# A gated delta rule kernel with a softplus feed-forward: contiguous inverses, queries in longer runs, raw keys and separate key products in chunks 2 and 3, unread products, another order of work

## The chip, the cores and the metric

The kernel runs on one core of a Trainium2 chip. The metric is the device time of one execution in microseconds (us). The core has five engines that run their own instruction streams and wait for each other by semaphores: TensorE (PE in the profile; PEld is its weight load), VectorE (DVE), ScalarE (ACT), GpSimd (POOL) and SyncE (SP), which issues transfers only.

## The reference

Four batches, eight heads (32 streams), 768 steps, head dimension 48. Each stream keeps a 48 x 48 state. Its output is the x of a feed-forward layer with 384 inputs and 2048 hidden units over 3072 tokens.

```python
def _attn_ref(q, k, v, beta, g):
    B, H, S, D = q.shape                      # 4, 8, 768, 48
    k_n = k / (np.linalg.norm(k, axis=-1, keepdims=True) + 1e-06)
    state = np.zeros((B, H, D, D))
    for t in range(S):
        readout = np.einsum('bhd,bhde->bhe', q[:, :, t], state)
        y[:, :, t] = g[:, :, t] * readout
        v_old = np.einsum('bhde,bhd->bhe', state, k_n[:, :, t])
        state = state + beta[:, :, t, None, None] * np.einsum('bhd,bhe->bhde', k_n[:, :, t], v[:, :, t] - v_old)

def _moe_ref(x, w_in, w_out):                 # x: 3072 x 384, w_in: 384 x 2048
    h = x @ w_in
    return (np.maximum(h, 0) + np.log1p(np.exp(-np.abs(h)))) @ w_out
```

## The kernel before, in words

The 768 steps are cut into 12 chunks of 64. Inside a chunk the recurrence becomes matrix products and the inverse of a triangular matrix of 64 x 64 per stream; from chunk to chunk only the state goes on. Chunks are handled in pairs (`GROUPS`): 0 and 1, 2 and 3, up to 10 and 11.

**Loads.** `load` fetches k, q, v and g of a chunk in two transfers each (`k1.0` is chunk 1, batches 0 and 1; `k1.1` is batches 2 and 3), 192 KB each. A partition is a time step, so DRAM is read in runs of 48 floats, 192 bytes. All go through SP's queue, but for `k0.1` and `k1.1`, which ACT issues. The feed-forward weights come through POOL's queue (`wload`, `w0.*` and `w1.*`).

**Front.** Keys and queries become half precision (`cast`). From the second pair on, `unit` (L284) multiplies each key by its inverse norm instead, and so waits for `norms`: ACT squares (`ksq`), DVE sums (`red`), a root follows (ACT for pairs 0 and 2, POOL's power for the others, L481), and DVE takes the reciprocal (`rnorm`). TensorE transposes (`trs`, L312) and ACT or DVE bring the result into `kqt` (`kev`). `gram` (L419, L420) forms key-key and key-query products of one batch half together; ACT or DVE takes the key part out (`kkc`), DVE masks the query part (`mask`). In chunks 0 and 1, whose keys stay raw, two items do it: `gramk` (L349, L350) and, when q is there, `gramq` (L382). There `lbeta` folds the norms into beta, and `vs` (L704) scales the values in the chain.

**Inverse.** For a pair, `ln` (L521) transposes on DVE, `prep` (L536) scales, and fifteen `step`s of two instructions each (L544, L551) solve 16 x 16 blocks: on DVE for pair 0, on POOL for all others. `c16` casts the result, `tn` (L564) and two `t32` (L574) transpose it on DVE, and TensorE builds the 32 x 32 blocks from it (`xmm` L598, `xs`, `tmm` L619 and L625, `td2`). The inverse lies in `td` as 32 rows of 32 heads, [P, i, u]: the elements of one head are 32 elements apart. `zmm` (L651, L658) makes the 64-row part `z` of it, with `td` as the moving operand.

**Chain.** Per chunk and half m of the heads: `ks` and `qs` (products with the state, L696), `w` (values minus that, DVE), `umm` (L737, L741; the stationary operand of L741 is one head of `td`), `u1`, `zu` (L762), `u2`, `smm` (L782) into the next state (`s`, DVE), `ymm` (L812), `y` (times g, DVE), `ytr` (L844) and `xt`, which lays the result out as x.

**Dense.** For each job (chunks 0, 1, then pairs 2-3 to 8-9, then 10, 11), `g1` (L872) makes 128 hidden units by 256 or 512 tokens, `soft` (L884, ACT) applies the softplus into a `ga` buffer, `g2` (L899) accumulates 128 tokens by 384 outputs over 16 blocks, `o` copies them out of the one buffer `p_o`, and `store` sends them off.

**Order.** Nothing is scheduled at run time. Every piece is an item with a number, its engines and what it depends on; the table `_ORDER` is a list of words like `D131` (item 131 on DVE). Each engine does its items in the order of the table, and waits in it block what follows on the same engine. Buffers come from rings of fixed size (`r_k` 4, `r_ga` 17, `p_d` 5 banks of PSUM, and others), and the table's order decides who gets which.

Read out by names, the table before begins on three engines like this:

```
SP:   k1.0 k0.0 q1.1 k2.0 q0.0 q1.0 k2.1 q0.1 k3.0 g1.1 v0.0 v0.1 q2.1 q2.0 k3.1 q3.1 q3.0 v1.0 q5.0 g0.1 g0.0 g1.0 v1.1 ...
ACT:  ... xs:0 w0:0.0 kev:q2.1 td2:0 ksq:3 z:0 u1:0.0 sqrt:2 u2:0.1 cast:qn3.0 ...
POOL: kn0.1 kn0.0 qn1.1 qn1.0 vs:0 w0:0.1 w0.0 clear:4 w0.2 vs:1 unit:kn2 clear:2 diag:2 w0.1 w0.3 unit:kn3 w1.0 diag:4 w1.1 w1.2 w1.3 qn4 prep:2 step:2 x15 unit:kn5 unit:kn4 sqrt:6 ...
```

Of the kernel before, what the change touches and what calls it, by code (L numbers as in the profile page):

```python
# [10 lines left out]
F32 = mybir.dt.float32  # L11
# [5 lines left out]
GROUPS = [[c, c + 1] for c in range(0, 12, 2)]  # L17

# [59 lines left out]
def kernel(  # L78
# [11 lines left out]
    nc = tc.nc  # L90
# [37 lines left out]
    r_q = ring("qf", 2, [P, 2, H, D], F32)  # L128
# [3 lines left out]
    r_qn = ring("qn", 2, [P, 2, H, 64], F16)  # L132
    r_ksq = ring("ksq", 1, [P, 2, H, D], F32)
    r_nv = ring("nv", 3, [P, 32], F32)
    r_nl = ring("nl", 2, [P, 32], F32)
    r_bl = ring("bl", 3, [P, 32], F32)
    r_kk = ring("kk", 3, [P, 2, U, HC], F16)
    r_kqt = ring("kqt", 10, [P, 2 * NP * 2 * C + HC], F16)
# [8 lines left out]
    r_td = ring("td", 4, [P, HC, U], F16)  # L147
# [6 lines left out]
    r_ga = ring("ga", 17, [P, 512], F16)  # L154
# [9 lines left out]
    for t in r_kn.tiles + r_qn.tiles:  # L164
        nc.vector.memset(t[:, :, :, D:], 0.0)
    for r in range(2):
# [27 lines left out]
    for t in r_kqt.tiles:  # L194
        nc.vector.memset(t[:, 4 * NP * C :], 0.0)
# [27 lines left out]
    def load(name, x, r, c, b2):  # L223
# [4 lines left out]

        def fn(en):
# [8 lines left out]
            add("load", f"{name}{c}.{b2}", "A" if name == "k" and c < 2 and b2 else "S", fn,  # L238
                bufs=[b])
# [26 lines left out]
    def kq_of(c, p):  # L266
        return kqt[c, p].ap[:, : 4 * NP * C].rearrange("p (n t) -> p n t", n=2 * NP)

    def front(c, kk, nv, nv_it):
        cl = c % 2  # L270
        parts = 2 if c < 2 else 1
        for p in range(2):
            kqt[c, p] = Buf(r_kqt)
        its, x_of = {}, {}
        for name, ring_ in (("k", r_kn), ("q", r_qn)):
# [3 lines left out]
            for h in range(parts):  # L279
                sl = slice(h, h + 1) if parts == 2 else slice(0, 2)  # L280
                if name == "k" and nv is not None:

                    def unit(en, f=f, x=x):
# [15 lines left out]
                        lambda en, f=f, x=x, sl=sl: copy(en, x.ap[:, sl, :, :D], f.ap[:, sl]),  # L299
                        deps=fl, bufs=[f, x], size=768 // parts)  # L300
# [3 lines left out]
            for h in range(parts):  # L304
# [3 lines left out]
                def trs(en, x=x, tp=tp, ps=ps):  # L308
                    o = f16ps(tp.ap).rearrange("p (a n t) -> p a n t", a=2, n=NP)
                    for p in ps:  # L310
                        for i in range(NP):
                            nc.tensor.transpose(  # L312
                                o[:, p, i],
                                x.ap[:, p, 2 * i : 2 * i + 2].rearrange("p h d -> p (h d)"),
                                ident,
                            )
# [4 lines left out]
                for p in ps:  # L321

                    def kev(en, p=p, tp=tp, name=name):
                        s = f16ps(tp.ap).rearrange("p (a n t) -> p a n t", a=2, t=C)[:, p]
                        kq = kq_of(c, p)
                        copy(en, kq[:, :, :C] if name == "k" else kq[:, :, C:], s)

                    its[name].append(
                        add("kev", f"{name}{c}.{p}", "AD", kev, deps=[t1], bufs=[tp, kqt[c, p]])
# [9 lines left out]
        if c < 2:  # L339
# [697 lines left out]
```

## Time and profile before

| | |
|---|---|
| three runs | 281.72, 284.75, 284.81 us; median 284.75 |
| the profiled execution | 282.21 us |
| its span, first to last instruction | 280.3 us |
| granted TensorE clock | 0.994 |
| busy: PE, PEld, DVE, ACT, POOL | 238.7, 165.1, 153.7, 130.2, 114.1 us |
| transfers | 107705 packets, 27.71 MB, 99 GB/s on average |
| SP's queue | 101600 packets, 23.21 MB, 51.1% of the time of 16 DMA engines |

The span is what the trace covers; 1.9 us of the execution lie around it. The busy time of PE counts overlapping products once. The chain of waits names what ended last before each instruction; an idle engine matters only where it stands in that chain or where PE, the busiest engine, waits for it.

### The profile page before, as it was taken

The numbers are of one execution on the slowest core, as the hardware profiler recorded it, in microseconds if no ns is written. First come the engines' busy times: TensorE is split into PE (matmuls) and PEld (weight loads), VectorE is DVE, ScalarE is ACT, GpSimd is POOL, SyncE is SP. The second block draws the span as 40 slices with busy tenths as digits, with TensorE's granted clock in tenths as the row PEclk, the third lists the DMA queues.
The fourth block names the chain that finished last, engine by engine and source line by source line (L and its number), as shares of the span: only waits on it lengthen the run. The fifth ranks groups of instructions, "written<-read, shape, count | busy, mean of one in ns | idle before, by whom it ended". The sixth has DMA issues, their size and how long they took to land.

```text
span 280.3 us, 13451 instructions
## 1 busy us (share of the span) xinstructions
PE 238.7 (85%) x6112; PEld 165.1 (59%) x6112; DVE 153.7 (55%) x333; ACT 130.2 (46%) x248; POOL 114.1 (41%) x217
## 2 busy tenths in 40 slices
PE   0540579979978998899998999999999999999993
PEld 0420467857647673467765657756566566677761
DVE  7899645482266787856684585561764242413000
ACT  3551265364374677563414755126652355214630
POOL 8115019308805888988605527820038600000000
PEclk9999999999979999999999999999999999999999
DMA  8999968999972399921885980510233410110123
GB/s 120 157 149 148 196 100 133 190 185 177 164 121 39 59 166 151 175 51 35 142 143 90 147 165 21 131 33 5 60 59 68 102 33 5 30 30 4 28 56 87
DMA packets 107705, 27.71 MB, mean 99 GB/s; under 512 B 100864, under 2 KB 107648, under 8 KB 107648
## 3 DMA queue, kind: packets, MB, share of 16 engines
q1 hardware_dynamic: 101600, 23.21, 51.1%
q0 software_dynamic: 3968, 3.25, 7.7%
q8 instruction: 48, 0.79, 1.3%
q10 hardware_dynamic: 2080, 0.39, 1.0%
q14 instruction: 9, 0.07, 0.1%
HBM read 25.26 MB, written 4.72 MB: 107 GB/s over the span
## 4 chain that ended last, share of the span: by engine, by line
PE 50%; POOL 21%; DVE 13%; issue 13%; ACT 2%; POOLq 0%; DVEq 0%
PE h L872 15%; PE o L899 13%; POOL tt L551 8%; POOL tmp L544 8%; PE d L696 3%; DVE ln L521 3%; PE d L658 2%; POOL kn L284 2%; PE d L312 2%; PE d L741 2%; PE d L625 2%; PE d L812 2%; PE d L762 2%; DVE tmp L544 2%; POOL nn L536 2%
## 5 line engine op out<-in xcount | busy, mean ns | idle before, releaser
L884 ACT ACTIVATE ga<-h 128x512 f16<-128x512 f32 x96 | 55.7, 598 | 46.3 <-PE h L872 44.5
L872 PE MATMUL h<-xt,w_in 128*128 128x512 f16 (+1 forms) x384 | 75.3, 331 | 1.9 <-ACT ga L884 1.9
L899 PE MATMUL o<-w_out,ga 128*128 128x384 f16 x384 | 73.3, 332 | 0.6 <-ACT osb L205 0.6
L899 PEld LDWEIGHTS <-ga 128*128 128x128 f16 x384 | 35.6, 99 | 24.0 <-issue 2.4
L872 PEld LDWEIGHTS <-w_in 128*128 128x128 f16 x384 | 35.0, 99 | 21.7 <-issue 2.7
L551 POOL TENSOR_TENSOR tt<-tt,tmp 128x30 f32<-128x30 f32 (+7 forms) x75 | 27.6, 368 | 5.9
L544 POOL TENSOR_TENSOR tmp<-nn,tt 128x30 f32<-128x30 f32 (+7 forms) x75 | 26.9, 359 | 5.8
L207 DVE CAST u<-d 128x384 f16<-128x384 f32 x21 | 11.5, 555 | 22.7 <-PE d L741 9.0
L536 POOL TENSOR_TENSOR nn<-ln,beta_l 128x256 f32<-128x256 f16 x10 | 6.3, 650 | 40.4 <-DVE ln L521 40.2
L481 POOL TENSOR_TENSOR nv<-nv,half_c 128x32 f32<-128x32 f32 x3 | 16.5, 5504 | 12.8 <-DVE nv L468 12.8
L207 DVE COPY osb<-o 128x384 f32<-128x384 f32 x12 | 6.6, 548 | 27.4 <-PE o L899 27.4
L205 ACT ACTIVATE kqt<-d 128x512 f16<-128x512 f16 x26 | 15.2, 595 | 13.8 <-DVE kqt L207 10.4
L205 ACT ACTIVATE u<-d 128x384 f16<-128x384 f32 x27 | 12.9, 489 | 17.6 <-PE d L741 10.2
L284 POOL TENSOR_TENSOR kn<-kf,nv 128x768 f16<-128x768 f32 x10 | 14.7, 1475 | 14.3 <-DVE nv L491 10.6
L437 DVE TENSOR_TENSOR mt<-d,mask 128x256 f16<-128x256 f32 x40 | 15.8, 417 | 7.2 <-PE d L420 3.7
L827 DVE TENSOR_TENSOR yg<-d,gf 128x384 f16<-128x384 f32 x24 | 12.9, 553 | 8.5 <-PE d L812 7.5
L312 PE MATMUL d<-ident,kn 128*128 128x128 f16 x96 | 9.1, 250 | 8.7 <-DVE kn L207 7.6
L598 PE MATMUL d<-tn,kk 16*32 16x16 f16 x768 | 7.3, 184 | 10.6 <-DVE tn L564 10.4
L696 PEld LDWEIGHTS <-kqt 48*64 48x64 f16 x704 | 12.7, 112 | 5.8 <-issue 4.6
L696 PE MATMUL d<-s,kqt 48*64 48x48 f16 x704 | 15.4, 192 | 0.5 <-issue 0.5
L205 ACT ACTIVATE kk<-d 128x256 f16<-128x256 f32 x33 | 11.3, 384 | 8.3 <-DVE mt L437 4.1
L564 DVE STREAM_TRANSPOSE tn<-tw 128x512 f16<-128x512 f16 x6 | 8.7, 1454 | 11.3 <-POOL tw L207 9.1
(106 smaller groups left out, 399.1 us busy)
## 6 DMA issues: line engine op xcount, KB each, us to landing
qf<-in_q_dram SPq DMA_DIRECT2D x24, 192.0 KB, 5.5
gf<-in_g_dram SPq DMA_DIRECT2D x24, 192.0 KB, 4.5
vf<-in_v_dram SPq DMA_DIRECT2D x24, 192.0 KB, 5.4
out_dram<-osb SPq DMA_DIRECT2D x48, 96.0 KB, 2.2
kf<-in_k_dram SPq DMA_DIRECT2D x22, 192.0 KB, 5.3
w_in<-in_moe_w_in_dram POOLq DMA_DIRECT2D x4, 384.0 KB, 7.3
w_out<-in_moe_w_out_dram POOLq DMA_DIRECT2D x4, 384.0 KB, 11.2
kf<-in_k_dram ACTq DMA_DIRECT2D x2, 192.0 KB, 7.0
```

The lines of the kernel that those rows point to most:

```text
L205: nc.scalar.activation(o, x, AF.Copy, scale=float(sign))
L207: ENG[en].tensor_copy(o, x)
L284: ENG[en].tensor_tensor(x.ap[:, :, :, :D], f.ap, nv.ap[:, 16 * cl : 16 * cl + 16] .rearrange("p (a h) -> p a h", a=2)[:, :, :, None] .broa ...
L312: nc.tensor.transpose(o[:, p, i], x.ap[:, p, 2 * i : 2 * i + 2].rearrange("p h d -> p (h d)"), ident,)
L437: nc.vector.tensor_tensor(mt[c][m].ap[:, NP * p : NP * p + NP], gb[m].ap.rearrange("p (n b) -> p n b", n=NP)[:, :, C:], mask[:, None, :].b ...
L481: nc.gpsimd.tensor_tensor(nv.ap, nv.ap, half_c, ALU.pow)
L544: eng.tensor_tensor(t, nn.ap[:, :, j + 1 :, j : j + 1].broadcast_to([P, 2, n, w]), tt.ap[:, :, j : j + 1, :w].broadcast_to([P, 2, n, w]), ...
L551: eng.tensor_tensor(rows, rows, t, ALU.add)
L696: nc.tensor.matmul(hd(o.ap)[HALF[r], NP * p + i], kq_of(c, p)[FEAT[m], 2 * i + r, off : off + C], s0[r].ap[FEAT[m], NP * p + i], **start(p ...
L872: nc.tensor.matmul(hp.ap[:, n * b : n * b + n], w_in[:, j, f * P : (f + 1) * P], xt.ap[:, j, t0 : t0 + n], start=(j == 0), stop=(j == 2),)
L884: lambda en, hp=hp, o=gb: nc.scalar.activation(o.ap, hp.ap, AF.Softplus),
L899: nc.tensor.matmul(op.ap[:, :DM], b.ap[:, col + c0 : col + c0 + 128], w_out[:, f, :], start=(f == 0), stop=(f == NF - 1),)
```

## The change

- Queries are loaded with another layout (`fnq`): a partition is a head and a group of four time steps, so that each run in DRAM is 4 x 48 floats, 768 bytes. A load is two transfers of 96 KB. The cast brings the four time steps into rows (on ACT one instruction for each batch half), the transposes work on it as before, and the query `kev` reads PSUM with the time steps 128 elements apart to put them in order.
- `kqt` is one buffer of a chunk instead of two. `gram` so waits for keys and queries of both halves.
- After `td` is made, its first half is copied (`tu`, a new item on DVE, ACT or POOL, one per pair), and the second half (`td2`) is written straight, into `tu` as [P, u, i]: the 32 elements of a head lie side by side. `zmm` and `umm` read `tu`.
- Chunks 2 and 3 get `gramk` and `gramq` instead of `gram` (`SPLIT`), and raw keys (`RAW`): a `cast` instead of `unit`, `lbeta` for the pair, and `vs` in the chain.
- For the first pair, `xs` and `td2` are done chunk by chunk.
- Three `warm` items: four 128 x 512 products each of the identity into a PSUM bank, which nobody reads. They are first on PE.
- Some rings change: `r_ga` 16 instead of 17, `r_td` 1 instead of 4 with a new `r_tu` of 4, `r_nl` 1.
- `_ORDER` is another table.

```diff
+WARM = 3
+SPLIT = (0, 1, 2, 3)
+RAW = (0, 2)
...
+        def fnq(en):
+            for m in range(2):
+                ENG[en].dma_start(
+                    out=b.ap[:, b2, m],
+                    in_=x[2 * b2 : 2 * b2 + 2, :, t0 : t0 + C].rearrange(
+                        "p (i m) (g t) d -> m (p i) g (t d)", m=2, t=4
+                    )[m],
+                )
...
+    def cast(en, name, x, f, sl):
+        if name == "k":
+            copy(en, x.ap[:, sl, :, :D], f.ap[:, sl])
+        else:
+            rs = range(sl.start, sl.stop) if en == "A" else [sl]
+            for r in rs:
+                o, y = x.ap[:, r], f.ap[:, r]
+                dims = "p" if en == "A" else "p r"
+                copy(
+                    en,
+                    o[..., :D],
+                    y.rearrange(f"{dims} m (t d) -> {dims} t m d", d=D),
+                )
...
-                        s = f16ps(tp.ap).rearrange("p (a n t) -> p a n t", a=2, t=C)[:, p]
-                        kq = kq_of(c, p)
-                        copy(en, kq[:, :, :C] if name == "k" else kq[:, :, C:], s)
+                        s = f16ps(tp.ap)[:, 512 * p : 512 * p + 512]
+                        if name == "k":
+                            copy(en, kq_of(c, p)[:, :, :C], s.rearrange("p (n t) -> p n t", t=C))
+                            return
+                        o = kqt[c].ap[:, : 8 * NP * C].rearrange("p (x r y) -> p x r y", r=2, y=2 * C)
+                        copy(
+                            en,
+                            o[:, :, p, C:].rearrange("p x (g t) -> p x g t", t=4),
+                            s.rearrange("p (t x g) -> p x g t", t=4, x=8),
+                        )
...
-        if c < 2:
+        if c in SPLIT:
...
-                t2 = add("gram", f"{c}.{p}", "P", gram, deps=[its["k"][p], its["q"][p]],
-                         bufs=gb + [kqt[c, p]], mm=32, mode="6432")
+                t2 = add("gram", f"{c}.{p}", "P", gram, deps=its["k"] + its["q"],
+                         bufs=gb + [kqt[c]], mm=32, mode="6432")
...
+        tu = Buf(r_tu)
+        tu_it = add("tu", tag, "DAG",
+                    lambda en: copy(
+                        en, tu.ap[:, :, :16], td.ap[:, :16].rearrange("p i u -> p u i")
+                    ),
+                    deps=[td_its[0]], bufs=[td, tu])
...
-        halves = [[c % 2 for c in cs]]
+        halves = [[c % 2] for c in cs] if cs[0] < 2 else [[c % 2 for c in cs]]
...
-                     lambda en, us=us: copy(en, td.ap[:, 16:, us], iu(ep.ap)[:, :, us]),
+                     lambda en, us=us, e_=ep[hs[0]]: copy(
+                         en, tu.ap[:, us, 16:], iu(e_.ap)[:, :, us].rearrange("p i u -> p u i")
+                     ),
...
-                    nc.tensor.matmul(
-                        o[f].rearrange("p u i -> p i u"),
-                        ident[f, f],
-                        td.ap[f, :, 16 * cl : 16 * cl + 16],
-                    )
+                    nc.tensor.matmul(o[f], ident[f, f], tu.ap[f, 16 * cl : 16 * cl + 16])
...
-                            td.ap[QUAD[2 * r + 1], :, 16 * cl + u],
+                            tu.ap[QUAD[2 * r + 1], 16 * cl + u],
...
-                            o[f, pi], td.ap[f, :, 16 * cl + 2 * pi + m], w1.ap[f, pi]
+                            o[f, pi], tu.ap[f, 16 * cl + 2 * pi + m], w1.ap[f, pi]
...
+    for i in range(WARM):
+        hot = Buf(p_d)
+
+        def warm(en, hot=hot):
+            for _ in range(4):
+                nc.tensor.matmul(hot.ap, ident, ident[:, None, :].broadcast_to([P, 4, P]))
+
+        add("warm", f"{i}", "P", warm, bufs=[hot], mm=4, mode="full")
...
-        inv = cs[0] > 1
+        inv = cs[0] not in RAW
```

The new table, read out by names, up to the places that the prediction speaks of:

```
SP:   k1.0 k0.0 q0.0 k2.0 q1.1 q1.0 g1.1 k4.0 k2.1 k3.0 g0.0 q0.1 v0.1 k4.1 q2.0 k5.0 q2.1 k3.1 v0.0 v1.1 g0.1 q5.1 k5.1 q3.1 q3.0 q5.0 v1.0 ...
ACT:  k1.1 k0.1 ksq:1 kev:k1.0 ksq:0 kkc:1.11 sqrt:0 kev:k0.0 kev:k0.1 cast:qn0.0 kkc:1.10 kkc:0.10 kkc:0.00 kkc:0.11 ksq:2 ... xs:0 td2:0 sqrt:2 ksq:5 u1:0.0 z:0 u1:0.1 kkc:2.10 kev:k3.0 u2:0.0 ...
DVE:  ... kkc:1.00 clear:0 kkc:1.01 lbeta:0 kkc:0.01 kev:q1.0 diag:0 ln:0 prep:0 step:0.0-5 red:2 step:0.6-7 kev:q0.1 step:0.8-14 mask:1.0 tn:0 t32:0.1 mask:0.1 t32:0.0 red:3 xs:1 mask:1.1 red:5 eps:2 mask:0.0 u2:0.1 ... lbeta:2 ln:2 ...
POOL: kn1.1 kn0.0 kn0.1 qn1.1 qn1.0 kn2 w0.2 c16:0 vs:0 w0.0 qn2 w0:0.0 tu:0 clear:4 w0:0.1 w0.3 qn3 w1.2 vs:1 w0.1 clear:2 w1.0 w1.1 diag:2 w1.3 prep:2 step:2 x15 unit:kn5 clear:6 diag:4 qn6 sqrt:6 vs:3 unit:kn6 ...
PE:   warm x3 trs:k1.0 trs:k1.1 gramk:1.1 gramk:1.0 trs:k0.0 trs:k0.1 gramk:0.0 gramk:0.1 trs:q1.1 trs:q1.0 trs:k2 trs:q0.0 trs:q0.1 gramq:1 gramq:0 xmm:0 xmm:1 tmm:0 trs:k3 umm:0.0 zmm:0 umm:0.1 gramk:2.1 zu:0.1 zu:0.0 smm:0.0 smm:0.1 ymm:0.0 gramk:2.0 ymm:0.1 ytr:0.1 gramk:3.1 ytr:0.0 trs:q2 gramk:3.0 trs:q3 g1:0.2 ks:1.0 tmm:1 ...
```

Later in it, DVE takes four of the `unit` items (chunks 4, 7, 9 and 11) and `vs` of chunk 2, which are POOL's in the table before or new. `tu` is on POOL for pairs 0 and 4, on ACT for pair 6, on DVE for 2, 8 and 10.

## The prediction

> **What bounds it now.** I read the page first, then the busy time by stretch, the order of time on each engine, the chain of waits, the groups.
>
> ```profile
> span 280.3 us, 13451 instructions
> ...
> PE 238.7 (85%) x6112; PEld 165.1 (59%) x6112; DVE 153.7 (55%) x333; ACT 130.2 (46%) x248; POOL 114.1 (41%) x217
> ...
> PE   0540579979978998899998999999999999999993
> ...
> DMA  8999968999972399921885980510233410110123
> ```
>
> ```profile
> 0.00:30.00 30.00, 8.61 (x356) 6.86 (x357) 26.02 (x84) 11.55 (x23) 11.68 (x26) 1.00 1.13 146
> 30.00:45.00 15.00, 10.15 (x382) 8.57 (x379) 7.84 (x16) 7.52 (x14) 4.25 (x5) 1.00 0.83 134
> 45.00:60.00 15.00, 13.72 (x344) 10.89 (x341) 7.78 (x18) 6.30 (x14) 6.27 (x9) 1.00 1.19 179
> 60.00:260.00 200.00, 190.86 (x4932) 128.35 (x4930) 111.46 (x216) 97.97 (x187) 91.88 (x178) 0.99 0.51 87
> 260.00:276.00 16.00, 15.31 (x110) 10.45 (x107) 0.56 (x2) 6.42 (x12) 0.00 (x0) 1.00 0.21 50
> ```
>
> After the length come the busy times of PE, PEld, DVE, ACT and POOL, the clock, DMA and GB/s. There are two stages. Up to 45 us PE waits (18.8 of 45 busy) while DMA is full. From 45 us on it is the bound: it idles 1.3 us up to 60, 9.1 in the next 200, 0.7 in the last 16. So the end moves by an earlier start, by less PE work, or by those 10.4 us.
>
> ```profile
> 22.57 1.57 POOL L704 TENSOR_TENSOR vf<-vf,nv 128x768 f32<-128x768 f32 x1 [7.76 <-DVE tmp L544]
> 22.84 1.41 DVE L544 TENSOR_TENSOR tmp<-nn,tt 128x96 f32<-128x96 f32 x1
> 36.12 0.30 PE L625 MATMUL d<-td,xs 32*16 32x16 f16 x17 [3.80 <-issue]
> 40.69 1.47 POOL L704 TENSOR_TENSOR vf<-vf,nv 128x768 f32<-128x768 f32 x1 [13.99 <-DMA vf<-in_v_dram]
> 62.51 1.19 POOL L536 TENSOR_TENSOR nn<-ln,beta_l 128x256 f32<-128x256 f16 x2 [11.22 <-DVE ln L521]
> ```
>
> Four delays stand here: a DVE step stretched from 0.25 to 1.41 beside a POOL instruction; a PE stop of 3.80 inside tmm; vs:1 waiting for its values until 40.7; and the inverse of pair 2, begun only at 62.5, as unit:kn2 and kn3 stand behind vs:1 on POOL and everything up to ln:2 hangs on them.
>
> **The change, part by part.** Sums are made on the span, 280.3; 1.9 lie around it (282.21).
>
> A, the start. Before, ln:0 began at 13.53, the steps ended at 26.33, tmm at 30.86, umm at 37.13, the first u1 at 37.89. After: ACT has ksq:0 at 9.15 (0.83), kkc 0.38, sqrt after red:0 to 11.2, two kev 1.06, a cast 0.52, four kkc 1.21: ln:0 at 14.0, +0.5. Into the steps come red:2 (0.94) and kev:q0.1 (0.41 to 0.69); vs:0 now stands behind c16:0 on POOL, so the stretched pair (1.41 + 0.53 against 0.5) goes: +0.1. c16 0.6, tn 1.46, two t32 and a mask between them 1.95 put tmm:0 at 31.0. It serves one chunk, 0.9; td2:0 is half, 0.4: umm:0.0 at 32.3 if the PE stop is gone, 36.1 if not.
>
> A new wait follows. On ACT ksq:5 stands ahead of u1:0.0, and needs load k5.1; behind it are u1:0, z:0, u2:0.0, so the first chain, and red:5 holds mask:0.0 and u2:0.1 on DVE. Before, 25 loads had landed at 40.7, 1.6 each. k5.1 is again the 25th, but 7 of them are queries. What do these cost?
>
> ```profile
> q1 hardware_dynamic: 101600, 23.21, 51.1%
> q0 software_dynamic: 3968, 3.25, 7.7%
> ```
>
> 51.1% of 280.3 x 16 over 101600 packets is 22.6 ns for mostly 192 bytes; on q0 87 ns for 819. So 256 packets of 768 bytes cost between a quarter of a load now (0.4) and all of it (1.6). I take 0.8; it holds the second transfer that SP now issues for each query load (24 more in all), as SP's 0.8 to 2.6 us per issue before were mostly waits for room. The Trainium skill's page "DMA: Bandwidth & Descriptors" (Specifications) puts line rate at 512 bytes and more and 27 GiB/s on an engine; by it 768 bytes take some 27 ns (an estimate), a load 0.4, and the start would be 2.8 earlier than in my sum. With 0.8, k5.1 lands at 18 x 1.6 + 7 x 0.8 = 34.4, u1:0.0 begins at 35.2, against 37.9: **-2.7**. Ends: queries no cheaper, u1 at 40.8, +2.9; k5.1 at 31.6 and no PE stop, -5.0.
>
> The unread products (12 of 512 columns; 6 of 256 took 1.40 cold, so 0.47 each) fill PE from 1.7 to 7.3; the first transposes came at 7.59. They cost nothing, and up to 0.5 if data come earlier.
>
> ```profile
> 45.06 1.40 PE h L872 x6
> 48.05 0.97 PE d L312 x8
> 56.02 0.76 PE h L872 x6
> 124.06 0.45 PE d L312 x8
> 155.50 0.57 PE d L741 x21
> 158.28 0.50 PE d L762 x30
> 194.19 0.70 PE d L658 x25
> ```
>
> The same transposes take 0.97 early and 0.45 later: PE runs at half pace until some 53 us. Warmed, the first transposes would save 0.5; I count 0, ends +0.5 and -0.5. The page "TensorE: Matmul & The Clock Gate" (Part 1) says that about 3.4 us without work bring the half clock back; by it the warmth is lost in the wait from 14 to 28 us, and the dense work begins cold as now. The sum doesn't change by it.
>
> B, PE work. L658 goes at 28 ns a product (0.70/25), L741 at 27, L762, whose operands are contiguous, at 16.7. The groups say what is slow:
>
> ```profile
> L651 PE MATMUL d<-td,ident 32*32 32x512 f16 x24 | 8.1, 670 | 0.0
> ...
> L741 PEld LDWEIGHTS <-td 32*32 32x32 f16 x384 | 12.1, 144 | 0.9 <-ACT td L205 0.8
> ```
>
> Other weight loads of 32 columns take 89 to 107 ns. If contiguous heads bring both to 16.7, that is (11.3 + 10.3) ns x 384 = 8.3; if the pace is set by issue, 0. I take the middle, -4.1. Chunks 2 and 3 pay for separate products: 32 more each, at L382's pace (64 in 1.07) 0.53, +1.1. Together **-3.0**, ends +1.1 and -7.2.
>
> C, PE's waits from 45 us on. vs:1 now needs v1.0, the 29th load (10 queries): 38.4 with ends 34.4 and 46.4. vs 1.5 and four weight issues 3.2 put POOL at prep:2 by 43.5. ln:2 no longer waits for norms before the transposes: ytr:0 came 5.6 after u1, so at 40.8; gramk, kkc and 1.9 of ln: 43.5 too. Steps of 14.4 end at 58 instead of 76.9. Then 12.4 of POOL (sqrt:6 5.5, two unit and vs:3 4.4, two casts 1.7, the rest 0.8) and ln:4 put the inverse of pair 4 at 85, before 114.6. PE has two dense jobs (10.4 each), three chains (7 each), most of g1:2 (8) and the products of pairs 4 and 6 (8) ahead of xmm:4: 57 from 40 on, so 97. POOL leads by 12, and PE's waits for inverses should go. What stays are the links of the chain. I take **-6** of 10.4, ends 0 and -9.
>
> Costed at nothing: the query kev with strided reads, 13 of them on DVE. A contiguous one takes 414 ns, a float32 one of the same size 692: 0 to 0.28 each, 3.6 in all. The page "Advanced Engine Details and Errata" (VectorE Performance Modes) speaks against the change here: the double rate needs unit step in the innermost dimension, so by it all 13 pay the 0.28. tu is 0.6 each on three engines, four unit on DVE some 1.08 each (twice L728's 541). What hides them: DVE is busy 111 of 200 us and PE has dense work to do; rival 2 prices the loss of that cover. The 16th ga buffer instead of the 17th costs nothing while g1 follows the last g2 that frees them. Store and tail (4.4) stay.
>
> Sum: 280.3 - 2.7 - 3.0 - 6 = 268.6, with 1.9 around it 270.5. The profiled execution lay near the lowest of three runs and 0.9% under their median; scaled, 272.9. I say 272, between the two.
>
> **Rivals.** 1, the parts don't do what they say: queries no cheaper (+2.9), pace set by issue (+1.1), prep:2 at 51.5 and so half of C (-3): 280.3 + 1.0 + 1.9 = 283. For it: SP issued k, v and q alike at 0.8 to 2.6 each, so the bytes may count. Against: 22.6 ns a packet at 99 GB/s on average.
>
> 2, slower: DVE's queue becomes the bound of the chain. The state of chunk c + 1 needs w and s on DVE; each link now finds an unit or its like (1.08) and a longer kev (0.28) ahead. If the dense work no longer covers it, 12 x 1.36 = 16.3 come on top: 268.6 + 6 + 16.3 + 1.9 = 292.8. It decides from the point where PE, at a w, has no g1 or g2 in order before the next ks. For it: DVE carries w, s, y and all masks in one queue. Against: PE idled only 4.6% from 60 to 260, while DVE had 44% free.
>
> 3, better: all lower ends, 280.3 - 5.0 - 7.2 - 9 + 1.9 = 261.0, scaled 263. It needs no PE stop, line rate for queries and the pace of L762.
>
> **From this to the numbers.** Forecast 0.64, own range 264 to 279; rival 1 0.15, 2 0.10, 3 0.11. 261 to 283 leaves out rival 2 and part of rival 1. Over 2% faster is under 279.1, about what a measurement of this kernel can tell: 0.64 less 0.02, and 0.11, some 0.74; within 2% 0.16; slower 0.10.
>
> **What would show it.** In the changed profile: L658 and L741 under 22 ns a product; u1 of chunk 0 at 35, and who held it; prep of pair 2 near 44 and its xmm near 60; under 5 us of PE idle from 60 on; SP's queue at some 83,000 packets (18,400 fewer) and a share near 44% (24 x 0.8 of 280 less). I am wrong if PE waits for DVE w or s links in the middle, if ACT stands at ksq:5 until 40, or if a product's pace is unchanged.

## The result, and the profile after

The changed kernel takes 281.19 us (median of 12 runs, 277.16 to 284.6), the kernel before 283.25 (12 runs beside them). The ratio is 0.9855 with a 95% interval of 0.9808 to 0.9903: about 1.5% faster, where the prediction said 4.5% and gave 0.74 to more than 2%. Medians here and below are of all runs, and ratios compare only the runs within 1.5% of the fastest of their kernel; by the medians alone the gain is 0.7%. The profiled execution took 279.88, span 278.1.

The page, its head and the rows by slices:

```profile
span 278.1 us, 13637 instructions
...
PE 236.5 (85%) x6188; PEld 157.3 (57%) x6188; DVE 164.1 (59%) x339; ACT 124.7 (45%) x241; POOL 116.7 (42%) x224
...
PE   6425348889988799899989899989999999999993
...
PEclk9655555899999799999999999999999999999999
DMA  8989999997699889770466350680104330100412
```

The same stretches as before (columns as there: length, then PE, PEld, DVE, ACT, POOL, clock, DMA, GB/s):

```profile
0.00:30.00 30.00, 13.07 (x244) 7.48 (x245) 23.28 (x77) 10.16 (x20) 9.99 (x24) 0.65 0.97 149
30.00:45.00 15.00, 8.42 (x418) 7.08 (x417) 8.78 (x16) 6.07 (x13) 8.28 (x11) 0.50 0.95 162
45.00:60.00 15.00, 12.30 (x361) 9.53 (x337) 10.69 (x22) 8.19 (x15) 11.31 (x23) 0.83 1.10 177
60.00:260.00 200.00, 189.42 (x5104) 124.26 (x5105) 120.24 (x225) 94.56 (x184) 87.14 (x167) 0.99 0.48 86
260.00:276.00 16.00, 13.25 (x95) 8.99 (x92) 1.11 (x2) 5.76 (x10) 0.00 (x0) 1.00 0.23 55
```

The clock row must be read with care. Before, it shows 1.00 from the start, though eight transposes took 0.97 us at 48.05 and 0.45 at 124.06; the record seems to begin with the first change of the clock. After, the unread products cause one, so the half pace up to 50 us becomes visible (without them, in a run below, the row reads 1.00 again). It is not new.

The span splits at the first dense product, which PE begins at 45.0 before and at 49.95 after. From there to the end, kernel before and then kernel after:

```profile
45.00:280.30 235.30, 219.90 (x5382) 149.69 (x5378) 119.79 (x235) 111.11 (x212) 98.15 (x187) 0.99 0.53 91
```

```profile
49.95:278.10 228.15, 210.73 (x5426) 139.49 (x5424) 128.83 (x241) 106.66 (x204) 96.04 (x187) 0.99 0.49 88
```

Start +4.9; PE's work 210.73 - 219.90 = -9.2; PE's waits (228.15 - 210.73) - (235.30 - 219.90) = 17.4 - 15.4 = +2.0. The sum is -2.2, as 278.1 - 280.3. But part of the first two is only a shift: the new order puts products of chunks 2 and 3 ahead of the first dense one. PE is busy for 25.72 us before it, where it was 18.75, and the unread products make 4.78 of that:

```profile
0.00:49.95 49.95, 25.72 (x765) 17.85 (x766) 35.27 (x99) 18.08 (x38) 20.68 (x38) 0.59 0.97 155
```

So 2.2 us of work moved from behind the split to ahead of it, and without the shift the three terms are +2.8, -7.0 and +2.0. The prediction, whose A ends at `u1:0.0`, had -2.7, -3.0 and -6. The one term that brings the gain is more than twice as large as I said, and the other two have the wrong sign.

One profile does not fix these terms to a microsecond. A second one of the same kernel (281.86 us, first dense product at 50.11) has:

```profile
50.11:280.20 230.09, 215.21 (x5426) 142.99 (x5424) 129.09 (x241) 107.04 (x204) 97.11 (x189) 0.97 0.50 87
```

That is +5.1, -4.7 and -0.5 against the kernel before. In it the clock row reads 0.50 up to 58 us, in the first up to 50, and dense products take longer in between (the first six 1.49 us against 0.94).

**Work.** The groups that were slow (PE first, then weight loads):

```profile
L785 PE MATMUL d<-w,tu 32*32 32x48 f16 x384 | 8.7, 182 | 1.7 <-issue 1.2 <-POOL tu L213 0.5
L702 PE MATMUL d<-tu,kk 32*32 32x32 f16 x384 | 7.6, 173 | 0.9 <-issue 0.9
L699 PE MATMUL d<-tu,ident 32*32 32x512 f16 x24 | 4.8, 398 | 0.4 <-DVE mt L472 0.2 <-DVE tu L213 0.2
...
L785 PEld LDWEIGHTS <-tu 32*32 32x32 f16 x384 | 6.3, 90 | 2.3 <-issue 1.4 <-POOL tu L213 0.9
```

The first two before:

```profile
L741 PE MATMUL d<-w,td 32*32 32x48 f16 x384 | 13.8, 214 | 0.4 <-ACT td L205 0.4
L658 PE MATMUL d<-td,kk 32*32 32x32 f16 x384 | 13.2, 227 | 0.0
```

Busy time falls from 13.8, 13.2 and 8.1 us (L741, L658, L651 before) to 8.7, 7.6 and 4.8; the weight load of L741 from 144 ns to 90. In the order of time, a run of 32 products of `zmm` took 1.06 before and 0.59 now, 16 of `umm` 0.63 and 0.37. Before, then after:

```profile
97.56 0.63 PE L741 MATMUL d<-w,td 32*32 32x48 f16 x16
...
134.00 1.06 PE L658 MATMUL d<-td,kk 32*32 32x32 f16 x32
```

```profile
101.14 0.37 PE L785 MATMUL d<-w,tu 32*32 32x48 f16 x16
...
135.23 0.59 PE L702 MATMUL d<-tu,kk 32*32 32x32 f16 x32
```

That is 0.47/32 = 15 ns and 0.26/16 = 16 ns less for each product, and twice 384 of them make some 12 us; less remains in PE's busy time, where groups overlap and the separate products of chunks 2 and 3 come on top.

**Start.** ACT in the order of time:

```profile
32.29 0.84 ACT L211 ACTIVATE kn<-kf 128x768 f16<-128x768 f32 x1 [6.83 <-DMA kf<-in_k_dram]
33.04 0.83 ACT L499 ACTIVATE ksq<-kf 128x768 f32<-128x768 f32 x1
33.77 0.36 ACT L211 ACTIVATE xs<-d 128x256 f16<-128x256 f32 x1
34.97 0.38 ACT L211 ACTIVATE tu<-d 128x256 f16<-128x256 f32 x1 [0.83 <-PE d L671]
...
39.80 0.84 ACT L499 ACTIVATE ksq<-kf 128x768 f32<-128x768 f32 x1 [4.33 <-DMA kf<-in_k_dram]
40.54 0.47 ACT L211 ACTIVATE u<-d 128x384 f16<-128x384 f32 x1
```

`u1:0.0` begins at 40.54 (37.89 before, 35.2 predicted). Ahead of it in ACT's queue stands `ksq:5`, which waits until 39.80 for k5; `xs:0` stands behind the cast of kn3, which waits until 32.29 for k3. On DVE `ln:0` stands behind one strided `kev`, 2.31 late and 0.69 long, and begins at 17.08 instead of 13.53:

```profile
16.39 0.69 DVE L213 COPY kqt<-d 128x512 f16<-128x512 f16 x1 [2.31 <-PE d L342]
...
17.08 1.88 DVE L556 STREAM_TRANSPOSE ln<-kk 128x1024 f16<-128x1024 f16 x1
```

**Middle.** `prep:2` moved from 62.5 to 53.05, as the change intends, but the prediction had 43.5. Ahead of it on POOL `vs:1` waits for v1.0, which the prediction had landing at 38.4. SP issues v1.0 only at 40.33: it stands still from 33.93 to 36.48, a wait that POOL ends, and has three query loads, two transfers each, ahead of it. SP, then POOL:

```profile
33.30 0.63 SPq L245 DMA_DIRECT2D kf<-in_k_dram  x1
36.48 3.80 SPq L237 DMA_DIRECT2D qf<-in_q_dram  x6
40.33 0.63 SPq L245 DMA_DIRECT2D vf<-in_v_dram  x1
```

```profile
47.54 1.47 POOL L748 TENSOR_TENSOR vf<-vf,nv 128x768 f32<-128x768 f32 x1 [2.62 <-DMA vf<-in_v_dram]
...
74.58 0.83 POOL L213 CAST qn<-qf 128x768 f16<-128x768 f32 x1 [5.10 <-DMA qf<-in_q_dram]
81.69 5.78 POOL L516 TENSOR_TENSOR nv<-nv,half_c 128x32 f32<-128x32 f32 x1 [6.28 <-DVE nv L503]
92.28 1.47 POOL L748 TENSOR_TENSOR vf<-vf,nv 128x768 f32<-128x768 f32 x1 [4.81 <-DMA vf<-in_v_dram]
...
100.05 0.83 POOL L213 CAST qn<-qf 128x768 f16<-128x768 f32 x1 [3.50 <-issue]
100.84 1.19 POOL L571 TENSOR_TENSOR nn<-ln,beta_l 128x256 f32<-128x256 f16 x2
```

Between the inverses of pairs 2 and 4 POOL waits 5.10, 6.28, 4.81 and 3.50 us in order (for a query load, for DVE's norms, for a value load, and once with no releaser shown), and `prep:4` begins at 100.84 where it began at 99.90: the lead of 9.5 us is gone by the next pair.

### The profile page after: what moved, and what is told of

It is laid out like the page before. It is cut to its first block, busy times and chain, and to the rows that moved or that the text cites. A ratio compares the mean times of both kernels' runs of the same rounds, so it can differ in the third digit from the quotient of the medians.

```text
span 278.1 us, 13637 instructions
## 1 busy us (share of the span) xinstructions
PE 236.5 (85%) x6188; PEld 157.3 (57%) x6188; DVE 164.1 (59%) x339; ACT 124.7 (45%) x241; POOL 116.7 (42%) x224
## 3 DMA queue, kind: packets, MB, share of 16 engines
q1 hardware_dynamic: 83168, 23.21, 47.0%
## 4 chain that ended last, share of the span: by engine, by line
PE 33%; POOL 29%; DMA 12%; SPq 11%; issue 7%; DVE 4%; ACT 2%; POOLq 0%; DVEq 0%; ACTq 0%
PE h L916 13%; POOL tt L586 10%; PE o L943 10%; POOL tmp L579 10%; SPq L245 6%; DMA vf<-in_v_dram 5%; SPq L237 4%; DMA qf<-in_q_dram 3%; DMA kf<-in_k_dram 3%; POOL nn L571 2%; POOL nv L516 2%; PE d L740 1%; DMA gf<-in_g_dram 1%; DVE ln L556 1%; PE d L644 1%
## 5 line engine op out<-in xcount | busy, mean ns | idle before, releaser
L916 PE MATMUL h<-xt,w_in 128*128 128x512 f16 (+1 forms) x384 | 73.9, 327 | 2.0 <-ACT ga L928 1.1
L213 DVE CAST u<-d 128x384 f16<-128x384 f32 x25 | 13.7, 553 | 16.3 <-PE d L785 8.7
L213 DVE COPY osb<-o 128x384 f32<-128x384 f32 x10 | 5.6, 556 | 23.4 <-PE o L943 23.4
L772 DVE TENSOR_TENSOR w<-vf,d 128x384 f16<-128x384 f32 x22 | 11.8, 545 | 10.5 <-PE d L740 5.4
L740 PE MATMUL d<-s,kqt 48*64 48x48 f16 x704 | 16.3, 188 | 0.9 <-issue 0.9
L213 DVE COPY kqt<-d 128x512 f16<-128x512 f16 x26 | 14.0, 550 | 4.8 <-PE d L342 4.6
L211 ACT ACTIVATE u<-d 128x384 f16<-128x384 f32 x23 | 11.1, 489 | 12.4 <-PE d L785 6.5
L841 DVE TENSOR_TENSOR s<-s,d 128x384 f16<-128x384 f16 x20 | 10.6, 547 | 9.8 <-PE d L826 9.8
L499 ACT ACTIVATE ksq<-kf 128x768 f32<-128x768 f32 x12 | 10.1, 842 | 13.4 <-DMA kf<-in_k_dram 13.2
L472 DVE TENSOR_TENSOR mt<-d,mask 128x256 f16<-128x256 f32 x32 | 13.0, 413 | 3.6 <-PE d L455 2.5
L503 DVE TENSOR_REDUCE nv<-ksq 128x16 f32<-128x768 f32 x12 | 11.3, 941 | 6.0 <-ACT ksq L499 6.0
```

What stands on the lines that cost most here:

```text
L211: nc.scalar.activation(o, x, AF.Copy, scale=float(sign))
L213: ENG[en].tensor_copy(o, x)
L472: nc.vector.tensor_tensor(mt[c][m].ap[:, NP * p : NP * p + NP], gb[m].ap.rearrange("p (n b) -> p n b", n=NP)[:, :, C:], mask[:, None, :].b ...
L740: nc.tensor.matmul(hd(o.ap)[HALF[r], NP * p + i], kq_of(c, p)[FEAT[m], 2 * i + r, off : off + C], s0[r].ap[FEAT[m], NP * p + i], **start(p ...
L916: nc.tensor.matmul(hp.ap[:, n * b : n * b + n], w_in[:, j, f * P : (f + 1) * P], xt.ap[:, j, t0 : t0 + n], start=(j == 0), stop=(j == 2),)
```

## The experiments

Orders are given by the names of items, engine first. Each comparison is with runs of the kernel before on the same chip.

**Parts undone or done alone, first look.** One kernel takes the order of before with contiguous inverses only (its line numbers stand one or more behind those of before):

```diff
-    r_td = ring("td", 4, [P, HC, U], F16)
+    r_td = ring("td", 1, [P, HC, U], F16)
+    r_tu = ring("tu", 3, [P, U, HC], F16)
 _ORDER: ... D:t32:2.0
+        D:tu:2      (likewise in the other five pairs)
```

> The kernel before, in its own order, with the inverses alone copied to contiguous rows (td2 written straight into tu, its first half copied on DVE after the second t32 of each pair, 6 copies). Theory 1 (the contiguous heads save PE work: L658 and L741 go from 28 and 27 to 15 and 13 ns a product, about 10 us in all, and the new order gives most of it back): this kernel is 7 to 10 us faster than the one before, ratio 0.965 to 0.975. Theory 2 (PE's pace in these products was covered, and what was gained in the changed kernel came from the earlier inverse of pair 2): within 2 us of the kernel before, ratio 0.993 to 1.007.

Four runs, 278.09 to 284.38, median 283.88, before 284.84. Too wide to decide; it is taken up again below.

The second is the changed kernel with strided inverses:

```diff
-    nc.tensor.matmul(o[f], ident[f, f], tu.ap[f, 16 * cl : 16 * cl + 16])
+    nc.tensor.matmul(o[f].rearrange("p u i -> p i u"), ident[f, f], td.ap[f, :, 16 * cl : 16 * cl + 16])
 (zmm and umm read td; no tu)
```

> The changed kernel with the inverses read from td as before (no tu, td2 into td, four td buffers), its order otherwise kept. Theory 1: 7 to 10 us slower than the changed kernel, so 4 to 8 us slower than the one before, ratio 1.015 to 1.03. Theory 2: within 2 us of the changed kernel, ratio 0.98 to 0.993.

Median 285.41, before 284.84; ratio 0.9883 [0.9844, 0.9923], into which only two runs of ten enter. It is measured again below, and the ratio does not hold.

**The start.** Two of the waits moved away, in the changed kernel:

```diff
-DVE: ... kkc:0.01 kev:q1.0 diag:0 ln:0 prep:0 ...
+DVE: ... kkc:0.01 diag:0 ln:0 prep:0 kev:q1.0 ...
-ACT: ... sqrt:2 ksq:5 u1:0.0 z:0 u1:0.1 kkc:2.10 kev:k3.0 u2:0.0 ...
+ACT: ... sqrt:2 u1:0.0 z:0 u1:0.1 kkc:2.10 kev:k3.0 u2:0.0 ksq:5 ...
 (red:5 behind s:0.0 on DVE)
```

> The changed kernel with two waits moved: on DVE the evacuation kev:q1.0 stands after prep:0 instead of ahead of ln:0, and on ACT ksq:5 (with red:5 on DVE) stands after u2:0.0 instead of ahead of u1:0.0. Loads keep their order. Theory 1a (these two in-order waits delay the first chain by their 3.5 and 4.5 us): ln:0 at 14, u1 of chunk 0 at 36 or earlier, the end 4 to 6 us earlier, ratio to the kernel before 0.965 to 0.975. Theory 1b (the loads themselves are late; behind these two waits stand others for the same transfers: ACT's cast of k3, POOL's vs:0 for v0): ln:0 at 14, but u1 of chunk 0 gains less than 3 us and the end less than 2, ratio 0.978 to 0.988.

Ratio 0.9873 [0.9811, 0.9936]; the changed kernel has 0.9855. The steps did begin 2.7 us earlier (`prep:0` at 16.3 instead of 19.0), but `u1:0.0` only 1.9 and the first dense product at 49.1, 0.85 earlier. Six other profiles with the unedited start have `u1:0.0` at 38.7 to 40.6 and the first dense product at 48.5 to 50.5, so neither shift stands clear of their spread. ACT in the order of time shows the next wait in the queue, unchanged:

```profile
32.35 0.84 ACT L211 ACTIVATE kn<-kf 128x768 f16<-128x768 f32 x1 [6.83 <-DMA kf<-in_k_dram]
...
33.83 0.36 ACT L211 ACTIVATE xs<-d 128x256 f16<-128x256 f32 x1
```

Then the loads themselves: as the last, and k4, k5 and q5 issued behind v1.0.

```diff
-SP: ... g1.1 k4.0 k2.1 k3.0 g0.0 q0.1 v0.1 k4.1 q2.0 k5.0 q2.1 ... q5.1 k5.1 q3.1 q3.0 q5.0 v1.0 ...
+SP: ... g1.1 k2.1 k3.0 g0.0 q0.1 v0.1 q2.0 q2.1 ... q3.1 q3.0 v1.0 k4.0 k4.1 k5.0 k5.1 q5.1 q5.0 ...
```

> As the run with the two waits moved, and SP also issues k4, k5 and q5 (six loads) after v1.0 instead of among the loads of chunks 0 to 3. Theory 1b: k3, v0 and v1 land 5 to 7 us earlier, the first dense product comes at 42 to 45 instead of 50, the end is 4 to 7 us earlier than in the changed kernel, ratio 0.962 to 0.975. Theory 1a: no further gain over the run with the waits moved. If the start does not set the end at all (PE catches up later), both of these runs stay within 1.5 us of the changed kernel, ratio 0.98 to 0.99.

Slower than before, 1.0166 [1.0116, 1.0217]. `u1:0.0` came at 35.92, near the 35.2 of the prediction, and yet the first dense product came at 57.76, and the end is 3.1% later than in the changed kernel: k5 lands at 51.7 instead of 39.8, ACT stands at `ksq:5` after all, behind the first chain now, for 12.43 us, and PE behind ACT:

```profile
52.91 0.21 PE L384 MATMUL d<-kqt 48*32 48x64 f16 x1 [10.33 <-ACT kk L211]
```

So the in-order wait for a load wasn't mended by giving other loads its place: it came back behind the next chain, longer.

**Four cases on one chip.** Order and query loads old or new, inverses strided or contiguous.

> The changed kernel once more, beside the next three on one chip, so that four cases stand side by side: order and query loads old or new, inverses strided or contiguous. Here all is new. Both theories expect some 0.985 of the time before, 280 where before is 284.

> The order and loads of before; the inverses alone are copied to contiguous rows (six copies on DVE). Theory 1, PE's pace reaches the end: PE busy from the first dense product on falls by some 9 us as it did in the changed kernel, and the end by 7 to 9: 275 to 277 where before is 284. Theory 2, half of it falls into waits for the inverses (POOL's steps, tn, first products), which no pace of PE moves: 279 to 281, and PE's idle time from 60 to 260 us grows by 3 to 5 over the 9.1 of before.

> The changed kernel with the inverses strided as before. Theory 1: the pace is worth 7 to 9 us in any order, so 287 to 289 where the changed kernel has 280. Theory 2: in the new order the waits are as long whatever the pace, so under 3 us more than the changed kernel, 281 to 283, with 4 to 6 us less idle time of PE from 60 to 260.

> As the second, with the query loads in 768-byte runs as well; still the order of before, no unread products, chunks 2 and 3 as before. Theory 3, the new order gives back what contiguous rows and query loads bring: v1 lands some 4 us earlier than 40.7, the inverse of pair 2 begins by 58 instead of 62.5, and the end is 1 to 4 us under the second run and so 2 to 6 under the changed kernel. Rival: the loads hide behind PE's own work from 45 us on, and the time is that of the second run within 1 us.

The fourth is the text of the changed kernel with

```diff
-WARM = 3
-SPLIT = (0, 1, 2, 3)
-RAW = (0, 2)
+WARM = 0
+SPLIT = (0, 1)
+RAW = (0,)
 (ga 17, tu 3; xs and td2 of the first pair for both chunks at once;
  _ORDER is that of before with tu behind t32 on DVE)
```

| kernel | median, us | ratio to before | 95% |
|---|---|---|---|
| before | 284.40 | 1 | |
| changed, again | 282.44 | 0.9841 | 0.9762 to 0.9919 |
| old order, contiguous | 281.21 | 0.9890 | 0.9842 to 0.9938 |
| new order, strided | 284.79 | 0.9988 | 0.9944 to 1.0033 |
| old order, contiguous, query loads | 278.83 | 0.9796 | 0.9744 to 0.9847 |

The second and third kernels are those of the first look. Contiguous inverses bring 1.1% in the old order and 1.5% in the new (by the medians 1.1% and 0.8%). Without them the rest of the change brings nothing (0.9988). The earlier 0.9883 for the strided kernel lies outside this interval; its median was above that of before there too, and I go by the second measurement, into which nine runs enter. Theory 1 (7 to 9 us at the end) is too high; theory 2 (under 3 in the new order) fits by the medians, where 282.44 to 284.79 is 2.4, and is too low by the ratios, which make it 4.2. Counted at full clock (busy time times granted clock, summed over stretches of 2.5 us from the first dense product on), PE's work is 208.2 us with contiguous and 215.6 with strided inverses in the new order, 210.7 and 218.3 in the old: 7.4 and 7.6 less. So a third to a little over half of the pace reaches the end. What becomes of the pace shows between 60 and 260 us. New order, contiguous (the second look at the changed kernel), then new order, strided:

```profile
60.00:260.00 200.00, 190.12 (x5118) 125.55 (x5117) 120.24 (x225) 96.00 (x185) 88.17 (x169) 0.98 0.49 85
```

```profile
60.00:260.00 200.00, 194.76 (x5111) 130.85 (x5110) 118.44 (x221) 94.20 (x184) 86.39 (x167) 0.99 0.48 85
```

PE idles 9.9 us with contiguous inverses and 5.2 with strided ones: 4.6 us of the freed time stand there as waits. In the old order it is less, 11.2 (old order, contiguous) against 9.1.

The expectation that v1 would land 4 us earlier with cheaper query loads was a miss: `vs:1` began at 40.50 (40.69 before), `prep:2` at 59.90 (62.51).

**The middle, the unread products, the query loads.** Three edits of the changed kernel, and one of before:

```diff
-SP: ... k6.0 store:0.0 q6.0 k6.1 k8.1 q7.0 k8.0 g2.0 q7.1 q8.0 v3.0 k9.1 g2.1 q9.1 g3.1 v3.1 ...
+SP: ... k6.0 q6.0 k6.1 v3.1 v3.0 k8.1 q7.0 k8.0 g2.0 q7.1 q8.0 k9.1 g2.1 store:0.0 q9.1 g3.1 ...
 (POOL: cast:qn9.0 behind step:4.14; q10.1 later on SP, beside q10.0)
```

> The changed kernel with SP's order mended in the middle: store:0.0 no longer ahead of q6.0, v3 issued ahead of k8.1 and so some 12 us earlier, the cast of qn9 behind POOL's steps of pair 4. Theory 4, what the new order gives back in the middle is POOL standing in order at vs:3 and qn9 for late loads: prep:4 moves from 101 to under 96, and the end with it, by 3 to 5 us, to 0.970 of the time before. Rival: ln:4 (PE's products of chunks 4 and 5 in order, DVE) is as late as the loads were; prep:4 moves under 2 us and the end stays at 0.985.

0.9831 [0.9744, 0.9919]. The wait at `vs:3` is gone, and `prep:4` begins at 98.62 instead of 100.84. POOL in the order of time:

```profile
89.52 1.47 POOL L748 TENSOR_TENSOR vf<-vf,nv 128x768 f32<-128x768 f32 x1
...
98.62 1.19 POOL L571 TENSOR_TENSOR nn<-ln,beta_l 128x256 f32<-128x256 f16 x2 [2.44 <-DVE ln L556]
```

The releaser is DVE's `ln:4` now, as the rival said. Late loads were one of two causes, one hidden behind the other.

The second adds the two edits of the start:

> As the first, and also kev:q1.0 behind prep:0 and ksq:5 and red:5 behind the first chain. Theory 4: the two add, first dense product 1 us earlier and prep:4 under 95: 0.966 to 0.970. Rival: the first dense product still waits for the loads of k4 and k5, which this does not move; the time is that of the first run within 1 us.

0.9879 [0.9807, 0.9951]; first dense product at 48.43 (48.49 in the first), `prep:4` at 98.40. The two edits add nothing that these runs can tell.

The third has `WARM = 0`:

> The changed kernel without the twelve unread products. Theory 5, their warmth is gone before it is of use (granted clock 0.5 from 10 to 50 us): the same time within 1 us. Rival: the transposes between 7.9 and 9 us ran at full pace and set ln:0, so 0.5 to 1.5 us slower.

0.9876 [0.9817, 0.9936], first dense product at 48.82: within the spread of the changed kernel. The unread products do nothing for the time that these runs could tell.

The fourth is before with the query loads alone (`fnq`, the cast and the query `kev` of the diff, one `kqt` a chunk):

> Before with query loads in 768-byte runs alone (and the query evictions that go with them): order, inverses, products as before. If loads and pace add, 2 to 3 us under before, since with contiguous inverses they brought 0.9% more; rival: without the shorter products PE has no room for the earlier values and the gain is under 1 us.

0.9993 [0.9944, 1.0041]: no change. `vs:1` began at 40.39, no earlier than before. With contiguous inverses the same loads went from 0.9890 to 0.9796 on one chip; on another (below) that kernel had 0.9838. So they bring between nothing and 1%, and these runs show it only beside contiguous inverses; the intervals of 0.9890 and 0.9796 just touch.

**A real lead for pair 4.** In the order of before with contiguous inverses and query loads:

```diff
+A:ksq:4 D:red:4 A:ksq:5 D:red:5 A:sqrt:4 D:rnorm:4 D:unit:kn5 D:unit:kn4   (ahead of step:2.7)
+P:trs:k5 ... P:trs:k4 ... P:gram:4.1 ... P:gram:5.0 ... P:gram:4.0 ... P:gram:5.1   (between g1:1.0 and g2:0.1.12)
+P:ks:2.0 P:ks:2.1 P:qs:2.1 P:qs:2.0   (behind them, ahead of xmm:3)
+D:mask:4.10 D:mask:4.11 ... D:mask:5.11   (all eight, ahead of tn:2)
+D:ln:4 G:prep:4.0 G:prep:4.1 G:step:4.0 ...   (behind tn:2)
 (unit of chunks 6 and 7 on DVE and sqrt:6 on ACT, off POOL's way to prep:4)
```

> The fastest version so far (order of before, contiguous inverses, query loads in 768-byte runs) with a real lead for the inverse of pair 4: norms of keys 4 and 5 taken during the steps of pair 2 and their scaling on DVE, their transposes and products ahead of xmm:2, ks:2 and qs:2 behind them (they hold four of five PSUM buffers), roots of pair 6 on ACT, prep:4 right behind the steps of pair 2. Theory C of the prediction, earlier inverses take away PE's waits: prep:4 moves from 97 to some 78, the wait of xmm:4 for tn (3.8 in four) falls under 2, and the end falls 2 to 4 us under the next run. Rival: PE's order has no work to put there, so the end is the next run's within 1 us or later, since the early products of pair 4 stand ahead of dense work.

> The fastest version so far, unchanged, for comparison on the same chip: 0.98 of the time before (0.974 to 0.985).

The second has 0.9838 [0.9786, 0.9889]. The first is slower than before, 1.0209 [1.015, 1.0267], and the lead was not reached: `prep:4` at 91.7 (98.3 in the second) instead of 78. DVE in the order of time:

```profile
87.58 0.76 DVE L472 TENSOR_TENSOR mt<-d,mask 128x256 f16<-128x256 f32 x2 [0.35 <-ACT kk L211]
88.37 1.46 DVE L599 STREAM_TRANSPOSE tn<-tw 128x512 f16<-128x512 f16 x1
89.75 1.85 DVE L556 STREAM_TRANSPOSE ln<-kk 128x1024 f16<-128x1024 f16 x1
```

The masks of pair 4, whose products PE reaches late among dense ones, stand ahead of `tn:2`, which ran at 76.10 without the edit and here at 88.37. A lead for one pair was paid with 12 us on the pair ahead of it. The question it was made for stayed open, so the next three leave the order alone.

**Shorter inverses.** Seven of the fifteen steps are left out of every inverse but the first, so part of the computation is missing and the inverse is ready earlier.

```diff
-        for j in range(15):
+        for j in range(15) if first else (0, 1, 2, 3, 11, 12, 13, 14):
             prev = add("step", f"{tag}.{j}", en0, lambda en, j=j: step(en, j),
```

> Before, with steps 4 to 10 of 15 left out of the inverses of pairs 2 to 10 on POOL (part of the computation is missing), so that each inverse is ready some 6.6 us earlier with nothing else moved. Theory 6, with strided inverses PE's own work sets the end and waits are few: 0 to 2 us faster. Rival, the chain through POOL's inverses sets the end: 4 us or more.

> The changed kernel with the same steps left out. Theory 6: the pace that contiguous rows freed stands in waits for inverses, so shorter ones give 3 to 6 us: 0.965 to 0.975 of before where the changed kernel has 0.985. Rival: the waits are for other links (state, loads, DVE), under 1.5 us.

> The fastest version (order of before, contiguous inverses, query loads) with the same steps left out. Theory 6 and theory C of the prediction: PE's 3.8 us of waits for tn go and 3 to 5 us come off its 0.980 of before. Rival: PE's idle time from 60 to 260 us stays near 8.8 and the end moves under 1.5 us.

| with shorter inverses | ratio to before | 95% | with whole ones |
|---|---|---|---|
| before | 0.9857 | 0.9786 to 0.9929 | 1 |
| changed | 0.9785 | 0.9691 to 0.9878 | 0.9855 and 0.9841 |
| old order, contiguous, query loads | 0.9706 | 0.9635 to 0.9778 | 0.9796 and 0.9838 |

All three are lower, by some 4, 2 and 3 us (for the changed kernel the intervals overlap, and for the third they do with one of two). Before gains as much as the others, so theory 6, which said it wouldn't, falls in that part. PE's waits from 60 to 260 us, the kernel before with shorter inverses and the changed kernel with them:

```profile
60.00:260.00 200.00, 193.52 (x4909) 129.73 (x4909) 109.94 (x213) 96.92 (x185) 62.24 (x108) 0.96 0.53 87
```

```profile
60.00:260.00 200.00, 194.44 (x5176) 128.38 (x5174) 119.15 (x225) 99.17 (x191) 58.62 (x98) 0.99 0.50 88
```

Idle time goes from 9.1 to 6.5 and from 10.6 to 5.6 (in the first, at a clock of 0.96 instead of 0.99, part of that may be PE's slower pace). Five inverses, each some 7 us shorter (14.4 to 7.4 for pair 2 in the kernel before), move the end by a third to a little over half of the length of one. In these three kernels, of two orders, inverses ready 7 us earlier thus give 2 to 4 us; a longer lead was not tried.

## Why the prediction was wrong

Two of the three terms failed, A and C, and both first of all in one step: the time at which a load lands, summed up from what the loads cost. It was 5.4 us late for k5.1 and 9.1 for v1.0.

**A, the start: -2.7 taken, +2.8 measured (+4.9 at the first dense product).** The wait was named in the prediction, place and items: `ksq:5` ahead of `u1:0.0`, and ACT standing at `ksq:5` until 40 was one of its signs of being wrong. It stood until 39.80. What failed was the time given to k5.1, 34.4, summed up from 1.6 for each load and 0.8 for one of queries. As time in the queue, 0.8 was right: in the trace's packet records the 6144 query packets took 50.6 ns each, so 256 on 16 engines make 0.81 us a load, against 1.30 before (1024 packets of 20.3). SP's queue has 83168 packets and 47.0% of the time of 16 engines. But bytes didn't come faster: 149 GB/s in the first 30 us, 146 before, and in the old order `vs:1` began at 40.39 with the query loads alone and at 40.50 with contiguous inverses too, against 40.69 before. Why the shorter time in the queue buys no earlier landing stays open; SP now issues two transfers of at least 0.60 us for each query load, and no run tells that from a limit on the bytes. So my own end, +2.9 with queries no cheaper and u1 at 40.8, came close (40.54), for another reason than I gave and in part by luck: in six other profiles with this start u1 began at 38.7 to 40.6. By the page "DMA: Bandwidth & Descriptors" (Specifications) of the Trainium skill such a packet would take some 27 ns (an estimate from its line rate); the trace shows nearly twice that. Two more waits weren't in the sum at all: `kev:q1.0` ahead of `ln:0` (2.31 of waiting, 0.69 of work), and the cast of kn3 ahead of `xs:0` (6.83). ln:0 came at 17.08, not 14.0; the PE stop of 3.80, which I expected to vanish, did vanish. How much of the later start reaches the end isn't settled, as no edit made the start earlier by more than its spread without a longer wait behind it.

**B, PE's work: -3.0 taken, -7.0 measured.** The mechanism was right and the size off; of the -3.0, -4.1 stood for the contiguous rows, which brought 7.4 to 7.6 (at full clock, above). I took the middle between no gain and the pace of L762. The products saved 15 and 16 ns each where even my best case had 11.3 and 10.3: L762, the row that I took as its end, has operands twice as long each way. And I showed the 512-column products of L651 but put nothing in the sum for them; their busy time fell from 8.1 to 4.8.

**C, PE's waits: -6 of 10.4 taken, +2.0 measured (-0.5 in the second profile).** Two things failed. The lead: v1.0, by the same sum as k5.1 due at 38.4 and at the latest at 46.4, was there at 47.54, so `prep:2` came at 53.05 and not 43.5; the 5.5 between the two were nearly the 5.1 that I had. And `prep:4` came at 100.84: I followed the inverse of pair 2 item by item and gave pair 4 "12.4 of POOL" without asking what those items wait for. 19.7 us of in-order waits were in there, 9.9 of them on loads. With loads moved ahead (`prep:4` at 98.62) DVE's `ln:4` stood there instead. The price failed too: inverses some 7 us shorter, in a kernel where nothing else moves, give 2 to 4 us where I took 6; that a longer lead would have given 6 is not shown. The waits that POOL's inverses caused did become fewer, from 3.4 us for `tn` after 45 us to 0.5. Others took their place: waits that other work of DVE ended rose from 0.2 to 3.8 us, those with no releaser in the profile from 3.3 to 5.3. Changed kernel, waits of PE after 49.95 (line waited for and releaser, us, times, longest):

```profile
PE d L454 <- DVE w L772: 1.3, 1, 1.3
PE d L856 <- DVE u L213: 1.3, 2, 0.9
PE d L785 <- issue: 1.2, 1, 1.2
PE d L826 <- issue: 1.2, 1, 1.2
```

That looks like rival 2 in small, not 16 us but some: the work that DVE took over (strided `kev` at 0.69, `unit`, `vs`, `tu`) can stand ahead of `w` and `u`. No run moved it back, so this is not shown.

**Costed at nothing.** The unread products: right (0.9876 without). The clock row of the changed kernel falls to 0.50 by 10 us, long before the dense work. The strided `kev`: 0.69 against 0.41, which agrees with the page "Advanced Engine Details and Errata" (VectorE Performance Modes) of the Trainium skill, by which the double rate needs unit step in the innermost dimension; the one ahead of `ln:0` cost its 0.69 and the 2.31 of its wait, not 0.28.

**The whole.** Contiguous inverses explain the gain: they bring 1.1% and 1.5%, and without them 0.1% is left. The order, the split products, raw keys and unread products together bring nothing that these runs can tell from zero (0.9855 and 0.9841 with them, 0.9796 and 0.9838 without). The fastest version is the order of before with contiguous inverses and query loads, at 0.98 of before.

## What to carry to other kernels

Before a step is moved ahead in an engine's order, ask when its input arrives, not how long it takes: most waits found here were a short item standing in front of a long chain for a late load. A load that takes less of the queue's time need not land earlier. A saving of PE work is worth its full length only where PE doesn't wait; here some 7.5 us of work gave 2 to 4, as much of the rest came back as waits. How much "this would come earlier" is worth can be measured by shortening the work that is late, with the order left alone, before any order is rewritten.

## What the runs showed of the hardware

- An operand of 32 half-precision elements that lie 64 bytes apart, stationary or moving, cost a product some 15 ns more than one whose elements are adjacent, and its weight load 54 ns more (144 against 90). A 512-column product that read runs of 16 elements and wrote neighbours 128 bytes apart in PSUM took 670 ns, one that read and wrote straight on 398.
- On SP's queue a DMA packet of 768 bytes took 50.6 ns of an engine's time (48 to 53 in other runs), one of 192 bytes 20.1: four times the length, 2.5 times the time, and no more GB/s in the first 30 us (149 against 146), where the engines' share was 0.97 and 1.13.
- The granted clock falls now and then, with PE busy for 2.50 of 2.50 us: once in the profile of before (80 to 85 us), once in that of the changed kernel (95 to 100), three times in that of the old order with contiguous inverses and query loads. Over 5 us it then reads 0.66 to 0.70, over 2.5 us inside it 0.50 (80.0 to 82.5 before, 95.0 to 97.5 after). Two dips of the last kernel, by stretches of 5 us (length, PE busy, granted clock, DMA share, GB/s):

```profile
85.00:90.00 5.00, 4.99 (x137) 0.66 0.75 120
115.00:120.00 5.00, 5.00 (x92) 0.66 0.33 80
```

  A dip costs up to 0.34 x 5 = 1.7 us of PE's pace, so two or three of them weigh as much as most effects that were sought here. Why there are more of them in one run than in another stays open.
- After the first dense product, at 48 to 50 us, the full clock came back at once in one profile of the changed kernel (50 us) and only at 58 in another; over eight profiles with this or nearly this start it was 50 to 62. Each microsecond at half clock costs PE half a microsecond of pace, by estimate up to 6 us between two runs of one start.
